# Attention with one group of products per chunk, every engine in its written order, splits a unit later and moved decoding

## The chip, the cores and the metric

One core of a Trainium2 chip runs the whole kernel as one program. The time is that of the device from start to end, in microseconds (us), median of several runs. TensorE (PE) does matrix products and transposes, VectorE (DVE), ScalarE (ACT) and GpSimd (POOL) work on elements, and SyncE (SP) issues most of the DMA transfers. Each engine runs its instructions in the order in which they stand, and waits on semaphores for the others.

## The reference

An attention over 2 batches, 8 heads, 576 positions and 64 features, followed by a dense layer with softplus, and by a mixture of 8 experts. Only the attention is touched by the change:

```python
q_rot, k_rot = (rotate(q), rotate(k))
scores = scale * np.matmul(q_rot, k_rot.transpose(0, 1, 3, 2))
scores = scores - np.max(scores, axis=-1, keepdims=True)
attn = np.exp(scores)
attn = attn / (np.sum(attn, axis=-1, keepdims=True) + 1e-09)
return np.matmul(attn, v).astype(np.float32)
...
x = np.ascontiguousarray(attn_out.transpose(0, 2, 1, 3)).reshape(B * S, H * D)
x = _moe_ref(x=x, **moe_kwargs)
return _moe2_ref(x=x, **moe2_kwargs)
```

rotate is the rotary embedding (RoPE) with cos and sin of the position. All arithmetic is held at float32 accuracy: where a product runs in the fast format, its operands are split into a high and a low half.

## The kernel before, in words

The attention works on 8 pairs of heads (2 batches of 4 pairs). A pair has five units: four of 128 query rows (0 to 3), each with scores for both heads, and a mixed unit "m", which holds the last 64 rows of both heads in one block. In batch 0 a pair's units come as 0, 1, 2, 3, m, in batch 1 as 2, 3, m, 0, 1. Two chunks of units share the product with the values: in batch 0 the units 0 and 1 (256 columns wide) and 2, 3 and m (320 wide); in batch 1 the units 2 and 3, and m, 0 and 1.

For a unit and a head, TensorE makes the scores s (s_mm, L261; L243 for the mixed one), VectorE takes the maximum m (s_max, L270), ScalarE the exponential P with its sum (s_exp, L283). One unit later TensorE transposes P in three blocks of three (t_steps, L352; the mixed unit has one block of four and one of one), and ScalarE or VectorE copies each block into pt (L96, L98). When a chunk's blocks are there, TensorE multiplies them with the values into pv (pv_mm, L396). The sums become reciprocals (norm, L304, L305), are spread along a row into R, are transposed (norm_out, L316), copied to rb (norm_in), and pv times rb is x (x_out, L405), which GpSimd splits into the halves xh and xl for the next layer.

Meanwhile the next pair is made ready: GpSimd does its RoPE (L134 to L137), TensorE transposes q and k (tq, L174), ScalarE takes the high half out of PSUM (L161, L165) and VectorE the low half (L220, called from do_later), and SyncE copies both into the stacked forms qs and ks by DMA (L227). In batch 1 weights of the next layer are also loaded and decoded (decode, L557 to L560 on VectorE; high, L565 on ScalarE; low, L569 on VectorE), at units given in the table W_AT.

What sets the order: the string ORDER gives the steps of one unit's turn (S scores, T transposes, M maximum, E exponential, H copies of blocks, J products, N scaling, K and L the low halves, W weights, Q preparation of the next pair), and PREP what Q does in each of the five turns of a pair. Within a turn the four engines TensorE, VectorE, ScalarE and SyncE keep the written order; GpSimd is left to the scheduler, and each turn is a section of its own. The transposes, q and k transposes and R transposes share a pool of three PSUM buffers (tag t); scores have two, pv has one.

Of the kernel before, what the change touches and what calls it, by code (L numbers as in the profile page):

```python
# [27 lines left out]
ORDER = "S0 R T0 M0 K H0 E0 S1 T1 M1 L E1 H1 W J T2 N H2 Q".split()  # L28

PREP = (("xR", "k", "q", "xvR", ""), ("k", "qR", "x", "vm", ""), ("k", "qR", "x", "v", "r"))  # L30
# [11 lines left out]
    ((0, 0), (18, 24, 25, 25, 26)), ((0, 1), (20, 26, 27, 27, 28)), ((1, 0), (25, 28, 29, 29, 30)),  # L42
    ((1, 1), (27, 30, 31, 31, 32)), ((2, 0), (29, 32, 33)), ((3, 0), (31, 34, 35)), ((2, 1), (33, 36, 37)),
# [16 lines left out]
class Attention:  # L60


    def __init__(self, tc, q, k, v, cst, xh, xl, pools):
# [3 lines left out]
        self.engines = {nc.tensor.engine, nc.vector.engine, nc.scalar.engine, nc.sync.engine}  # L67
        self.pr = {}
        self.rem, self.rot = {}, {}
# [61 lines left out]
    def _rope(self, engs, out, x, tmp, cos, sin):  # L131

        e1, e2, e3 = engs
        e1.tensor_mul(out, x, cos)  # L134
        e2.tensor_mul(tmp[..., 0:32], x[..., 32:64], sin[..., 0:32])
        e2.tensor_mul(tmp[..., 32:64], x[..., 0:32], sin[..., 32:64])
        e3.tensor_add(out, out, tmp)  # L137

    def rope_rem(self, b, engs):
        self.rot[b] = self.nat.tile([128, H, D], F32, name=f"remr{b}", tag="remr", bufs=1)  # L140
        tmp = self.nat.tile([128, H, D], F32, name=f"remt{b}", tag="rtmp", bufs=2)
        c, s = (self.cst[x].unsqueeze(1).to_broadcast([128, H, D]) for x in ("cosr", "sinr"))
        self._rope(engs, self.rot[b], self.rem[b], tmp, c, s)

    def rope_pair(self, b, hp, i, engs):
        p = self.pr[b, hp]
        if "rot" not in p:
            p["rot"] = self.nat.tile([128, 2, 4, 2, D], F32, name=f"rot{b}{hp}", tag="rot", bufs=1)
        tmp = self.nat.tile([128, 2, 4, D], F32, name=f"rt{b}{hp}{i}", tag="rtmp", bufs=2)
# [3 lines left out]
        rot = p["rot"][:, i].rearrange("p j h d -> p h j d")  # L153
        self._rope(engs, rot, p["xn"][:, i], tmp, c, s)
# [145 lines left out]
    def norm(self, b, hp, c):  # L300
# [18 lines left out]
    def norm_in(self, b, hp, c, ps):  # L319
# [9 lines left out]
        self.x_out(b, hp, c)  # L329
# [70 lines left out]
    def x_out(self, b, hp, c):  # L400
# [26 lines left out]
    def run(self, side=None):  # L427
# [7 lines left out]
        with self.tc.manual_schedule(engines=self.engines):  # L435
            self.warm(0)
            for i in range(2):
                self.rope_pair(0, 0, i, (nc.vector,) * 3)
                self.tq(0, 0, i)
                self.warm(1 + i)  # L440
            self.rope_rem(0, (nc.vector,) * 3)
            low_q, _, low_k, _ = self.later
            self.later = []
            low_q()
            low_k()
            self.tr(0, True)
            self.warm(3)
        units = [(b, hp, u) for (b, hp) in pairs for u in self.order[b]]
        n = len(units)
        jobs = []  # L450
        for i in range(n + 4):
# [4 lines left out]
            with self.tc.manual_schedule(engines=self.engines):  # L456
                for step in ORDER:
                    g = int(step[1]) if len(step) > 1 else 0
# [5 lines left out]
                    elif step[0] == "S" and act:  # L464
                        self.s_mm(*cur, g)
                        if (i, g) == (0, 1):
                            self.warm(4)
# [948 lines left out]
def attention_moe_moe_kernel(ctx: ExitStack, tc, q, k, v, w_in, w_out, w_skip, w_gate, w1, w2, tab, out):  # L1416
    nc = tc.nc
# [205 lines left out]
```

## Time and profile before

| | |
|---|---|
| time, median of 3 runs | 493.01 us (492.19 to 493.56) |
| profiled execution | 493.06 us |
| its span | 491.2 us |
| mean granted TensorE clock | 0.998 |
| PE busy | 471.3 us (96%) |
| DVE busy | 371.8 us (76%) |
| ACT busy | 332.3 us (68%) |
| POOL busy | 130.6 us (27%) |
| attention, first scores to first hidden product | 12.65 to 165.1 us |

The durations in the rows are those of one profiled execution; the span leaves out some 1.9 us around it. A row of the time line gives start and duration of one instruction, or of several alike merged (x4), and in brackets how long the engine idled before it and who released it. One f32 product shows as two matmuls. A matmul's end is modelled, so what one piece costs TensorE is read from the start of one row to the start of the next. Rows of the mixed unit start a "pair" here: the mixed unit's scores of pair 0 stand at 28.44 us, of pair 3 at 82.91, of pair 4 (the first of batch 1) at 92.99, and of the last pair at 149.11. In rows 1 below the columns are: stretch, its length, then PE, PEld, DVE, ACT and POOL busy (us, with the instructions), the granted clock, the DMA share and GB/s.

### The profile page before, as it was taken

Reading aid. Unit: us, or ns where it says so; the run is one execution under the profiler, and the core shown is the slowest. Engines: PE = TensorE matmul, PEld = TensorE weight load, DVE = VectorE, ACT = ScalarE, POOL = GpSimd, SP = SyncE. Lnnn points to the kernel's source line nnn. Section 1 sums busy time; section 2 is a strip of 40 time slices with the busy share of each in tenths; the row PEclk is TensorE's granted clock in tenths of the full one; section 3 lists DMA queues with packets and bytes.
Section 4 is the critical chain, followed back from the end, with each engine's and each line's share of the span. In section 5 each row is a group of like instructions: output and inputs, shape, how many; then the busy total and the mean of one; then the engine's idle time right before and its main releaser. Section 6 shows DMA issues by size and latency. Waiting matters only on the chain. (4 is left out here: it accounts for less than half of the span.)

```text
span 491.2 us, 8838 instructions
## 1 busy us (share of the span) xinstructions
PE 471.3 (96%) x3054; PEld 382.1 (78%) x3055; DVE 371.8 (76%) x699; ACT 332.3 (68%) x782; POOL 130.6 (27%) x166
## 2 busy tenths in 40 slices
PE   7999999999999999999999999999999999999994
PEld 3777777766777678999998898899897768677683
DVE  7666776688996796799988995454886688979563
ACT  2667776676877677876678677765685458957550
POOL 0966785766131400000000000000110152551002
PEclk9999999999999999999999999999999999999999
DMA  7477547458462240223344241420335545895231
GB/s 186 152 194 195 121 123 200 95 161 208 101 177 77 97 129 1 87 63 113 125 129 125 91 129 44 140 75 2 99 100 203 228 111 194 285 311 224 78 120 39
DMA packets 41509, 65.49 MB, mean 133 GB/s; under 512 B 9087, under 2 KB 23679, under 8 KB 41456
## 3 DMA queue, kind: packets, MB, share of 16 engines
q1 hardware_dynamic: 38480, 59.99, 40.0%
q0 software_dynamic: 1344, 4.20, 2.7%
q10 hardware_dynamic: 1632, 0.66, 0.6%
q8 instruction: 26, 0.43, 0.4%
q14 instruction: 27, 0.22, 0.1%
HBM read 67.32 MB, written 6.76 MB: 151 GB/s over the span
## 5 line engine op out<-in xcount | busy, mean ns | idle before, releaser
L591 PE MATMUL h<-xh,w 128*128 128x320 f32 (+2 forms) x464 | 104.2, 309 | 0.8 <-ACT rb L96 0.8
L629 PE MATMUL acc<-w,gh 128*128 128x512 f32 x288 | 80.8, 397 | 1.3 <-ACT gh L619 1.3
L591 PEld LDWEIGHTS h<-xh,w 128*128 128x128 f32 x464 | 78.1, 188 | 4.7 <-ACT rb L96 1.1
L591 PE MATMUL h<-xl,w 128*128 128x320 f32 (+2 forms) x232 | 69.2, 308 | 0.0
L270 DVE TENSOR_REDUCE m<-s 128x1 f32<-128x576 f32 x64 | 48.0, 754 | 19.5 <-PE s L261 16.1
L629 PEld LDWEIGHTS acc<-w,gh 128*128 128x128 f32 x288 | 51.8, 188 | 12.0 <-ACT gh L619 3.2
L283 ACT ACTIVATE P<-s,m 128x576 f32<-128x576 f32 x64 | 47.6, 749 | 12.3 <-DVE m L270 10.7
L705 POOL TENSOR_SCALAR sc<-lg 128x2 f32<-128x2 f32 (+1 forms) x3 | 0.9, 293 | 201.8 <-DVE lg L688 201.8
L973 DVE TENSOR_TENSOR ws<-raw,ws 128x1024 fp32r<-128x1024 f32 x42 | 49.4, 1219 | 6.6 <-ACT ws L966 6.1
L604 ACT ACTIVATE y<-h 128x320 f32<-128x320 f32 (+2 forms) x58 | 25.4, 438 | 41.1 <-PE h L591 39.9
L352 PE MATMUL t<-ct,P 128*128 128x128 f32 x288 | 45.5, 277 | 2.5 <-ACT pt L96 2.5
L629 PE MATMUL acc<-w,gl 128*128 128x512 f32 x144 | 45.9, 392 | 0.0
L966 ACT CAST ws<-raw 128x1024 fp32r<-128x1024 f32 x42 | 42.0, 1051 | 5.2 <-DMA raw<-in_moe_w_dram 5.0
L620 DVE TENSOR_TENSOR gl<-r,gh 128x256 fp32r<-128x256 f32 (+2 forms) x42 | 25.8, 614 | 26.0 <-ACT gh L619 25.8
L261 PE MATMUL s<-ks,qs 128*128 128x288 f32 x224 | 43.7, 317 | 1.8 <-ACT P L283 1.7
L591 PEld LDWEIGHTS h<-xl,w 128*128 128x128 f32 x232 | 43.2, 188 | 2.0
L352 PEld LDWEIGHTS t<-ct,P 128*128 128x128 f32 x288 | 33.6, 140 | 9.6 <-issue 3.5
L96 ACT COPY pt<-t 128x384 f32<-128x384 f32 x60 | 28.1, 480 | 18.0 <-PE t L352 17.9
L396 PE MATMUL pv<-pt,vr 128*64 128x256 f32 (+1 forms) x256 | 37.1, 412 | 0.0
L638 PE MATMUL y<-ws,hT 128*128 128x512 f32 (+1 forms) x150 | 37.0, 392 | 0.0
L261 PEld LDWEIGHTS s<-ks,qs 128*128 128x128 f32 x224 | 31.6, 189 | 6.6 <-ACT P L283 3.6
L638 PE MATMUL mh<-ws,xgT 128*128 128x512 f32 x132 | 36.6, 418 | 0.0
(305 smaller groups left out, 946.1 us busy)
## 6 DMA issues: line engine op xcount, KB each, us to landing
raw<-in_moe_w_dram SPq DMA_DIRECT2D x56, 512.0 KB
raw<-in_moe_w_in_dram SPq DMA_DIRECT2D x16, 512.0 KB
raw<-in_moe_w_out_dram SPq DMA_DIRECT2D x16, 512.0 KB
sraw<-in_moe_w_dram SPq DMA_DIRECT2D x16, 512.0 KB
ks<-kT SPq DMA_DIRECT2D x28, 288.0 KB
qs<-qT SPq DMA_DIRECT2D x28, 128.0 KB
wr<-in_moe_w_dram SPq DMA_DIRECT2D x5, 512.0 KB
x2d<-x SPq DMA_DIRECT2D x9, 256.0 KB
```

The costliest lines, as they stand in the source:

```text
L96: self.nc.scalar.copy(out, in_)
L261: nc.tensor.matmul(ps[:, c, 0:288], lhsT=qs[:, a, uc], rhs=ks[:, a, x, 288 * c : 288 * c + 288], start=x == 0, stop=x == 1,)
L270: self.last = nc.vector.tensor_reduce(st["m"][:, a : a + 1], st["ps"][a][:, :, 0:288], axis=AX.XY, op=ALU.max, negate=True)
L283: nc.scalar.activation(P[:, 576 * a : 576 * a + 576].rearrange("p (c n) -> p c n", c=2), ps[:, :, 0:288], AF.Exp, bias=m[:, a : a + 1], ac ...
L352: self.tail = nc.tensor.transpose(ps[:, 128 * i : 128 * i + 128], src, ident)
L396: nc.tensor.matmul(ps[r, 0:n], lhsT=v, rhs=pt[:, k, 0:n], start=i < 0, stop=i == 3, skip_group_check=True,)
L591: nc.tensor.matmul(ps[c][:, 0:m], lhsT=w[:, 0, x, 128 * k : 128 * k + 128], rhs=src[:, k, c0 + m * c : c0 + m * c + m], start=z == 0, stop ...
L620: self.last = nc.vector.tensor_sub(gl, r, gh.bitcast(F32))
L629: nc.tensor.matmul(acc[t], lhsT=g[x][:, 128 * j : 128 * j + 128], rhs=w[:, 1, y, :], start=f == f0 and z == 0, stop=f == f1 and z == 2,)
L638: mm()
L966: self.nc.scalar.copy(self.w[T, c][:, 0], self.raw[c] if raw is None else raw)
L973: self.nc.vector.tensor_sub(w[:, 1], self.raw[c] if raw is None else raw, w[:, 0].bitcast(F32))
```

## The change

- The products of a chunk stand in one group in one turn (step J), followed by the transposes of the reciprocals. Before, they stood as two half groups in two turns, with a block of transposes behind the first half.
- All three blocks of transposes stand ahead of J, and the copies H1 and H2 too.
- The scaling (N and X) comes at the start of the next turn, and the split into xh and xl (Y) a turn after that.
- VectorE instead of GpSimd spreads the reciprocals into R.
- RoPE of a coming pair is cut into its single instructions, and the table ROPE says how many of them each turn takes (step G); the rotated q and k have two buffers instead of one. The q transposes stand one turn later (PREP).
- The turns of decoding and loading (W_AT) are others, and decoding stands whole in one turn.
- One section of written order holds the whole attention, and GpSimd is in it too.

```diff
-ORDER = "S0 R T0 M0 K H0 E0 S1 T1 M1 L E1 H1 W J T2 N H2 Q".split()
-
-PREP = (("xR", "k", "q", "xvR", ""), ("k", "qR", "x", "vm", ""), ("k", "qR", "x", "v", "r"))
+ORDER = "S0 R N T0 Y G M0 X K H0 E0 S1 T1 T2 M1 L E1 H1 H2 W J Q".split()
+
+PREP = (("xR", "k", "q", "xvR", ""), ("k", "R", "qx", "vm", ""), ("k", "R", "qx", "v", "r"))
+
+ROPE = ((0, 8, 0, 0, 4), (2, 2, 2, 2, 4), (2, 2, 2, 2, 0))
...
-    ((0, 0), (18, 24, 25, 25, 26)), ((0, 1), (20, 26, 27, 27, 28)), ((1, 0), (25, 28, 29, 29, 30)),
-    ((1, 1), (27, 30, 31, 31, 32)), ((2, 0), (29, 32, 33)), ((3, 0), (31, 34, 35)), ((2, 1), (33, 36, 37)),
+    ((0, 0), (18, 23, 23, 24, 26)), ((0, 1), (20, 26, 26, 27, 28)), ((1, 0), (24, 28, 28, 29, 31)),
+    ((1, 1), (27, 31, 31, 32, 33)), ((2, 0), (29, 33, 33)), ((3, 0), (32, 36, 36)), ((2, 1), (34, 38, 38)),
...
-        self.engines = {nc.tensor.engine, nc.vector.engine, nc.scalar.engine, nc.sync.engine}
+        self.engines = {nc.tensor.engine, nc.vector.engine, nc.scalar.engine, nc.sync.engine, nc.gpsimd.engine}
...
-        e1.tensor_mul(out, x, cos)
-        e2.tensor_mul(tmp[..., 0:32], x[..., 32:64], sin[..., 0:32])
-        e2.tensor_mul(tmp[..., 32:64], x[..., 0:32], sin[..., 32:64])
-        e3.tensor_add(out, out, tmp)
+        return [
+            lambda: e1.tensor_mul(out(), x, cos),
+            lambda: e2.tensor_mul(tmp()[..., 0:32], x[..., 32:64], sin[..., 0:32]),
+            lambda: e2.tensor_mul(tmp()[..., 32:64], x[..., 0:32], sin[..., 32:64]),
+            lambda: e3.tensor_add(out(), out(), tmp()),
+        ]
...
+                p["rot"] = self.nat.tile([128, 2, 4, 2, D], F32, name=f"rot{b}{hp}", tag="rot", bufs=2)
...
+    def ropes(self, n=None):
+
+        for _ in range(len(self.off) if n is None else min(n, len(self.off))):
+            self.off.pop(0)()
...
-            self.cp("g", R[:, 64 * k0 : 64 * k0 + k * d].rearrange("p (a d) -> p a d", a=k), x)
+            self.cp("v", R[:, 64 * k0 : 64 * k0 + k * d].rearrange("p (a d) -> p a d", a=k), x)
...
-        self.x_out(b, hp, c)
...
-    def pv_mm(self, b, hp, c, z):
+    def pv_mm(self, b, hp, c):
         nc, p, pt, n = self.nc, self.pr[b, hp], self.pt[b, hp, c], self.width(b, c)
-        if z == 0:
-            self.pv[b, hp, c] = self.ps_pv.tile([128, 512], F32, name=f"pv{b}{hp}{c}", tag="pv")
-        ps = self.pv[b, hp, c]
-        for i in ((-1, 0, 1), (2, 3))[z]:
+        ps = self.pv[b, hp, c] = self.ps_pv.tile([128, 512], F32, name=f"pv{b}{hp}{c}", tag="pv")
+        for i in range(-1, 4):
...
+        return partial(self.x_split, x, xh, xl)
+
+    def x_split(self, x, xh, xl):
         self.cp("g", xh, x)
-        nc.gpsimd.tensor_sub(xl, x, xh.bitcast(F32))
...
+        jobs, scale, split = [], None, []
+        for i in range(n + 2):
             cur = units[i] if i < n else None
             prev = units[i - 1] if 0 < i <= n else None
-            T, evs, scale = None, [None] * 3, None
+            T, evs = None, [None] * 3
...
+                if step == "R":
+                    T = self.t_steps(*prev) if prev else None
+                    if ready:
+                        self.norm(*ready[0])
...
+                elif step == "J" and ready:
+                    job = ready.pop(0)
+                    self.pv_mm(*job)
+                    scale = self.norm_out(*job)
+                    if i >= n:
                         scale()
-                    elif step in "KL":
-                        if (step == "K") == (0 < i < 5):
-                            self.do_later()
-                    elif step == "W" and side:
-                        side(i)
-                    elif step == "Q" and cur:
-                        self.prepare(i, pairs)
-                        if i == 1:
-                            self.warm(5)
+                        self.x_out(*job)()
+                        scale = None
+                elif step == "G":
+                    self.ropes(ROPE[min(i // 5, 2)][i % 5])
+                elif step == "Y" and split:
+                    split.pop()()
+                elif step == "N" and scale:
+                    scale()
+                elif step == "X" and scale:
+                    split.append(self.x_out(*scale.args[:3]))
+                    if i >= n:
+                        split.pop()()
+                    scale = None
...
-                        jobs += [(b, hp, c, z) for z in range(2)]
-        assert not jobs
+                        jobs.append((b, hp, c))
...
+                self.off += self.rope_pair(*nx, 1, g3) + self.rope_pair(*nx, 0, g3)
...
-            att.run(side)
+            with tc.manual_schedule(engines=att.engines):
+                att.run(side)
```

Three places show how the instructions move. The first is TensorE from the second scores of unit 1 (the first row) in the pair after "01m", batch 0: t is a block of transposes, pv the products, t01n the transposes of reciprocals, tq the q transposes. Before:

```order
L261 MATMUL s_812<-ks_513,qs_574 128x288 x4
L352 MATMUL t_817<-ct,P_766 128x128 x3
L396 MATMUL pv_829<-pt_654,vd_105 64x320 x2
L396 MATMUL pv_829<-pt_654,vr_127 64x320 x4
L352 MATMUL t_836<-ct,P_766 128x128 x3
L261 MATMUL s_863<-ks_513,qs_574 128x288 x4
L174 MATMUL tq_841<-ct,rot_576 128x128 x4
L352 MATMUL t_868<-ct,P_810 128x128 x3
L261 MATMUL s_878<-ks_513,qs_574 128x288 x4
L352 MATMUL t_883<-ct,P_810 128x128 x3
L396 MATMUL pv_829<-pt_654,vr_127 64x320 x4
L316 MATMUL t01n_899<-ct,R_800 128x128 x3
```

and in the changed kernel, from the same scores:

```order
L287 MATMUL s_776<-ks_493,qs_603 128x288 x4
L377 MATMUL t_781<-ct,P_731 128x128 x3
L377 MATMUL t_785<-ct,P_731 128x128 x3
L419 MATMUL pv_798<-pt_613,vd_105 64x320 x2
L419 MATMUL pv_798<-pt_613,vr_129 64x320 x8
L342 MATMUL t01n_809<-ct,R_762 128x128 x3
L287 MATMUL s_813<-ks_493,qs_603 128x288 x4
L377 MATMUL t_822<-ct,P_774 128x128 x3
L287 MATMUL s_838<-ks_493,qs_603 128x288 x4
L377 MATMUL t_843<-ct,P_774 128x128 x3
L377 MATMUL t_847<-ct,P_774 128x128 x3
L200 MATMUL tq_855<-ct,rot_568 128x128 x4
```

The third block (t_836 before, t_785 now) went from behind the first products to ahead of them, and the second half of the products from behind unit 2's blocks into the one group.

The second is ScalarE at the same place: the exponential of unit 0's second head, the small copies of the mixed block (t01m), the cast of the k transposes, then the first block's copy and unit 1's exponentials. Before:

```order
L283 ACTIVATE P_766,sm_767<-s_769,m_762 128x576
L96 COPY pt_654<-t01m_774 64x64 x2
L165 CAST kT_785<-tq_780 128x512
L96 COPY pt_797<-t_803 128x3x128
L283 ACTIVATE P_810,sm_767<-s_792,m_807 128x576
L283 ACTIVATE P_810,sm_767<-s_812,m_807 128x576
L96 COPY pt_797<-t_836 128x3x128
L161 ACTIVATE qT_846<-tq_841 128x512
```

and now:

```order
L309 ACTIVATE P_731,sm_732<-s_734,m_727 128x576
L98 COPY pt_613<-t01m_739 64x64 x2
L191 CAST kT_750<-tq_745 128x512
L98 COPY pt_759<-t_765 128x3x128
L309 ACTIVATE P_774,sm_732<-s_754,m_771 128x576
L309 ACTIVATE P_774,sm_732<-s_776,m_771 128x576
L98 COPY pt_759<-t_785 128x3x128
L98 COPY rb_818<-t01n_809 128x256
```

The rows up to the copy of the third block (t_836, t_785) stand alike; behind it the scaling's copies rb follow, and the q activation, which stood there, comes a turn later.

The third is VectorE from the mixed unit's maximum on (m01m), with the copy of a block, the reciprocals, x, and the copies of the mixed block. Before:

```order
L270 TENSOR_REDUCE m01m<-s01m_709 128x1
L98 COPY pt_654<-t_726 128x3x128
L304 TENSOR_SCALAR sm_603<-sm_603 128x5
L305 RECIPROCAL sm_603<-sm_603 128x5
L270 TENSOR_REDUCE m_762<-s_752 128x1
L405 TENSOR_TENSOR x_744<-pv_680,rb_742 128x256
L98 COPY pt_654<-t01m_757 128x4x64 x2
L270 TENSOR_REDUCE m_762<-s_769 128x1
```

and now:

```order
L296 TENSOR_REDUCE m01m<-s01m_675 128x1
L428 TENSOR_TENSOR x_695<-pv_653,rb_682 128x256
L100 COPY pt_613<-t_701 128x3x128
L296 TENSOR_REDUCE m_727<-s_711 128x1
L100 COPY pt_613<-t01m_716 128x4x64 x2
L296 TENSOR_REDUCE m_727<-s_734 128x1
L330 TENSOR_SCALAR sm_578<-sm_578 128x5
L331 RECIPROCAL sm_578<-sm_578 128x5
L100 COPY R_762<-sm_578 128x256
L100 COPY R_762<-sm_578 128x128
```

x now stands right behind the mixed maximum, the reciprocals moved behind the maxima of unit 0, and two new copies to R follow them.

## Rows read from the trace of the kernel before

**Rows 1.** Stretches of the attention and of what follows: busy time of each engine.
```profile
28.44:82.91 54.47, 52.47 (x404) 40.77 (x402) 39.65 (x76) 40.22 (x107) 38.78 (x53) 1.00 0.61 157
82.91:92.99 10.08, 9.61 (x75) 7.42 (x72) 7.92 (x16) 6.72 (x18) 5.15 (x10) 1.00 0.30 88
92.99:149.11 56.12, 52.69 (x396) 39.87 (x393) 47.92 (x91) 41.44 (x108) 26.55 (x35) 1.00 0.64 168
149.11:165.10 15.99, 15.02 (x114) 10.37 (x111) 10.44 (x23) 11.39 (x30) 3.50 (x7) 1.00 0.11 34
165.10:460.00 294.90, 292.75 (x1752) 249.82 (x1753) 231.31 (x437) 210.23 (x478) 34.72 (x34) 1.00 0.39 129
```

**Rows 2.** Waits of PE in the attention: us in total, times, longest.
```profile
PE t L352 <- ACT pt L96: 2.5, 3, 1.0
```

**Rows 3.** Time line of PE around products of a chunk.
```profile
54.24 0.76 PE L396 MATMUL pv<-pt,vd 128*64 128x320 f32 x4
...
56.01 0.55 PE L352 MATMUL t<-ct,P 128*128 128x128 f32 x3
...
57.36 0.49 PE L352 MATMUL t<-ct,P 128*128 128x128 f32 x3
57.61 0.78 PE L261 MATMUL s<-ks,qs 128*128 128x288 f32 x4
58.23 0.49 PE L352 MATMUL t<-ct,P 128*128 128x128 f32 x3
58.65 1.30 PE L396 MATMUL pv<-pt,vr 128*64 128x320 f32 x8
59.88 0.55 PE L316 MATMUL t01n<-ct,R 128*128 128x128 f32 x3
...
160.87 0.76 PE L396 MATMUL pv<-pt,vd 128*64 128x320 f32 x4
...
163.71 0.55 PE L316 MATMUL t13n<-ct,R 128*128 128x128 f32 x3
```

**Rows 4.** Time line of DVE, ACT and PE behind the mixed unit of pair 0.
```profile
29.51 0.76 DVE L270 TENSOR_REDUCE m00m<-s00m 128x1 f32<-128x576 f32 x1 [0.16 <-PE s00m L243]
30.36 0.74 ACT L283 ACTIVATE P00m<-s00m,m00m 128x576 f32<-128x576 f32 x1
...
34.53 0.74 ACT L283 ACTIVATE P<-s,m 128x576 f32<-128x576 f32 x1 [0.83 <-DVE m L270]
35.41 0.80 PE L261 MATMUL s<-ks,qs 128*128 128x288 f32 x4 [0.54 <-ACT P L283]
35.70 0.58 ACT L165 CAST kT<-tq 128x512 fp32r<-128x512 f32 x1
36.18 0.48 ACT L96 COPY pt<-t 128x384 f32<-128x384 f32 x1
```

**Rows 5.** Groups of DVE in the attention: busy us, mean ns, idle before.
```profile
L98 DVE COPY pt<-t 128x384 f32<-128x384 f32 x36 | 19.6, 548 | 3.1 <-PE t L352 3.1
...
L405 DVE TENSOR_TENSOR x<-pv,rb 128x256 f32<-128x256 f32 x8 | 3.3, 409 | 0.1
...
L98 DVE COPY pt<-t01m 128x256 f32<-128x256 f32 x2 | 0.7, 412 | 0.0
```

**Rows 6.** Time line of PE and ACT before the mixed unit of pair 0.
```profile
26.21 0.55 PE L352 MATMUL t<-ct,P 128*128 128x128 f32 x3
...
26.45 0.59 ACT L161 ACTIVATE qT<-tq 128x512 fp32r<-128x512 f32 x1
```

**Rows 7.** Time line of POOL and DVE; the adds' durations: ns min/median/max.
```profile
85.67 0.73 POOL L135 TENSOR_TENSOR rt<-xn,cr 128x256 f32<-128x256 f32 x1 [2.53 <-DMA xn<-in_k_dram]
...
85.70 0.73 DVE L304 TENSOR_SCALAR sm<-sm 128x5 f32<-128x5 f32 x1 [0.49 <-ACT P03m L283]
...
L304 DVE TENSOR_SCALAR sm<-sm x16: 157/170/730, 19.9 to 159.3; 128x4 f32<-128x4 f32 x8, 128x5 f32<-128x5 f32 x8
```

**Rows 8.** SyncE's DMA issues of the stacked q.
```profile
59.07 3.81 SPq L227 DMA_DIRECT2D qs<-qT  x4
```

More of the change, by code (lines that the diff above doesn't have):

```diff
@@ L152, in rope_pair @@
         )
-        rot = p["rot"][:, i].rearrange("p j h d -> p h j d")
-        self._rope(engs, rot, p["xn"][:, i], tmp, c, s)
+        return self._rope(engs, out, p["xn"][:, i], tmp, c, s)
+    def ropes(self, n=None):
+        for _ in range(len(self.off) if n is None else min(n, len(self.off))):
+            self.off.pop(0)()
     def halves(self, hi, lo, src, q=False):
@@ L405, in x_out @@
         nc.vector.tensor_mul(x, ps[:, 0:n], self.rb[b, hp, c][:, 0:n])
+        return partial(self.x_split, x, xh, xl)
+    def x_split(self, x, xh, xl):
         self.cp("g", xh, x)
-        nc.gpsimd.tensor_sub(xl, x, xh.bitcast(F32))
+        self.nc.gpsimd.tensor_sub(xl, x, xh.bitcast(F32))
     def warm(self, part):
@@ L434, in run @@
         self.load_v(*pairs[1])
[L435 to L447, printed above, removed]
+        self.warm(0)
@@ L448, in run @@
+        for i in range(2):
+            some(self.rope_pair(0, 0, i, (nc.vector,) * 3))
+            self.tq(0, 0, i)
+            self.warm(1 + i)
+        some(self.rope_rem(0, (nc.vector,) * 3))
+        low_q, _, low_k, _ = self.later
+        self.later = []
+        low_q()
+        low_k()
+        self.tr(0, True)
+        self.warm(3)
         units = [(b, hp, u) for (b, hp) in pairs for u in self.order[b]]
         n = len(units)
-        jobs = []
-        for i in range(n + 4):
+        jobs, scale, split = [], None, []
@@ new lines, in run @@
+            for step in ORDER:
+                g = int(step[1]) if len(step) > 1 else 0
+                act = cur and (g == 0 or cur[2] != "m")
+                if step == "R":
+                    T = self.t_steps(*prev) if prev else None
+                    if ready:
+                        self.norm(*ready[0])
+                elif step[0] == "S" and act:
+                    self.s_mm(*cur, g)
+                    if (i, g) == (0, 1):
+                        self.warm(4)
+                elif step[0] == "M" and act:
+                    self.s_max(*cur, g)
+                elif step[0] == "E" and act:
+                    self.s_exp(*cur, g)
+                elif step[0] == "T" and T and T[g]:
+                    evs[g] = T[g]()
+                elif step[0] == "H" and evs[g]:
+                    evs[g]()
+                elif step == "J" and ready:
[3 more added lines that the diff above has]
+                    if i >= n:
+                        scale()
+                        self.x_out(*job)()
[11 more added lines that the diff above has]
+                    scale = None
+                elif step in "KL":
+                    if (step == "K") == (0 < i < 5):
+                        self.do_later()
+                elif step == "W" and side:
+                    side(i)
+                elif step == "Q" and cur:
+                    self.prepare(i, pairs)
+                    if i == 1:
+                        self.warm(5)
@@ L495, in run @@
                     if ch[-1] == u:
-                        jobs += [(b, hp, c, z) for z in range(2)]
-        assert not jobs
+                        jobs.append((b, hp, c))
+        assert not jobs and not split and not scale and not self.off
     def prepare(self, i, pairs):
@@ L521, in prepare @@
             if step == "r" and n2 == (1, 0):
+                assert 1 in self.rot
                 self.tr(1)
```

54 lines of the change are left out of this document (18 added, 36 removed).

## The prediction, made before the changed kernel ran

> **What bounds the kernel now.** I read the mean clock and the stretches first, then TensorE's waits, then its rows in order. The granted clock is 1.00 in every stretch [rows 1], so no part of this is a clock matter. From 165.1 to 460 us TensorE is busy 292.75 of 294.90 us: whatever time the attention part saves or loses reaches the end one for one, since the instructions behind it stand in the same order as before. In the attention part the reader sees 52.47 of 54.47 us busy for three pairs of heads, and 52.69 of 56.12 us for the last three, where VectorE is at 47.92: the first are bound by TensorE, the last also by VectorE, which decodes weights there. TensorE's longest sum of waits in the attention part is 2.5 us, for ScalarE's copies of transposed blocks [rows 2]; its idle time from 28.44 to 165.1 us is 2.0, 0.5, 3.4 and 1.0 in the four stretches [rows 1], some 7 us. So the change can win what TensorE does not have to do, and part of these 7 us, and can lose whatever cover its new order takes from the chains of VectorE and ScalarE.
>
> **One group of products: the gain.** In one pair the products of a 320-wide chunk take 1.77 us for the first group (54.24 to 56.01) and 1.23 for the second (58.65 to 59.88), 3.00 together; the last chunk of the kernel, whose two groups already stand back to back, takes 2.84 (160.87 to 163.71) [rows 3]. Joining saves 0.16. Three transposes ahead of products cost 0.42 (58.23 to 58.65), ahead of scores 0.25 (57.36 to 57.61): one such change of kind goes, 0.17, and one behind a group (56.01 is followed 0.30 later), 0.05. That is 0.38 a chunk, and 15 of the 16 chunks have it: 5.7 us of TensorE's work.
>
> **The waits that the order makes.** Before, each half group stood between transposes and scores of other units and covered the chains of the other two engines. Now a unit with products holds all of them at its end and the others hold none. I walk one pair of batch 0 from the mixed unit's scores at 0. Durations: its maximum starts 1.07 later and its exponential 0.85 after that; TensorE may use an exponential 0.88 after its start (34.53 to 35.41); an exponential and two small copies take ScalarE 1.17 (34.53 to 35.70), a cast 0.48, and a copy is free for TensorE 0.55 after its start (0.48 and an estimated 0.07) [rows 4]. An ordinary maximum starts 0.8 after its scores (1.07 less the two products that the mixed unit has more, an estimate), and its exponential 0.78 after that. VectorE takes 0.76 for a maximum [rows 4], 0.55 and 0.41 for a block's and a mixed block's copy, 0.41 for x [rows 5], each some 0.07 less in a queue (the cast and the copy after it overlap by 0.1).
> - TensorE: scores 0.87, nine transposes 0.75, scores of unit 0 to 2.24. The mixed block's transposes need its exponential: 1.92 + 0.88 = 2.80. Wait 0.55.
> - VectorE in its written order: mixed maximum 1.07, x 1.75, copy 2.09, maximum 2.57, two copies of the mixed block 3.44 (0.64 after its transposes), second maximum 4.14. Its exponential starts at 4.92 and the second scores of unit 1 at 5.80, where TensorE has been free since 5.25. Wait 0.55.
> - ScalarE behind that exponential: two small copies, the cast of k at 6.09, and only at 6.57 the copy of unit 0's first block. The third block takes that one's buffer, since the three buffers of this pool hold this block, the second one and the k transposes whose low half is still to come. So it starts at 7.12 and not at 6.67. Wait 0.45. Before, the half group stood ahead of this block and hid it.
> - Then products, 7.54 to 10.38, and three transposes of reciprocals to 10.68.
> - From there to the next mixed unit the same walk gives waits of 0.05 (first scores of unit 3), 0.2 (its first block, for VectorE's copy behind x and a maximum), 0.1, and 0.4 (its third block, for the copy behind the q activation), and ends at 18.5.
> Three pairs: 18.5 twice, and 19.5 for the third, where 1.0 us of casts of the remainder stands ahead of two exponentials: 56.5 against 54.47, **+2.0**. The piece up to batch 1: 10.7 against 10.08, **+0.6** [rows 1].
>
> **Batch 1.** The same walk gives some 18.3 a pair, of it 2.1 waits: 0.3 for the q transposes (buffer), 0.7 for the scores behind the unit in which VectorE decodes (busy until about 7.8), 0.8 for a first block that waits for ScalarE's copy of the unit before, 0.3 for two others. The last pair has no q and k transposes, 17.5. Together 54.1 against 56.12, **-2.0**: here the moved decoding does help, since it now stands in units with products.
>
> **Start.** In pair 0 the q activation waits for the last scores that read the old q, which end where the transposes of 26.21 us follow, and runs at 26.45 [rows 6]. It now stands ahead of the copy whose buffer the third block needs: 26.45 + 0.48 + 0.55 = 27.48, where the block would have followed at 26.46 (26.21 and 0.25). Then 0.42, the whole group (320-wide 2.84, so 256-wide about 2.3) and 0.22: the mixed unit starts at 30.4, against 28.44, **+1.9**; its share of the products is back at the end.
> **End.** From the last mixed unit to the first hidden product 15.99 before. The last copies now come as in the walk, products at 11.4 to 14.25, and the first hidden product 1.38 after (163.71 to 165.10): 15.6, **-0.4**.
>
> **Costed at nothing.** Spreading reciprocals on VectorE: no row shows such a copy; from below it is nothing, from above 0.55, the copy of a larger block out of PSUM [rows 5], 24 times at most 13 us of VectorE; I take 0.3, 7 us. They stand in the units with products, where VectorE waits for TensorE; uncovered they would cost 0.3 to 0.6 a chunk. There GpSimd stands in the way: a 5-wide add took VectorE 0.73 us, from 85.70 to 86.43, while a GpSimd multiply ran from 85.67 to 86.40; the median of these adds is 0.17 [rows 7], so it waited 0.56. I allow the same for a spread: two in a chunk stay under the 2.84 of the products. The splits a unit later, RoPE in pieces and its second buffer: GpSimd is 26.55 of 56.12 busy, 38.78 of 54.47 earlier, less the spreads now; what waits for it (q and k transposes) comes over 4 us later by the walk. If not, each of 14 would cost up to one piece. The first raw loads leave the crowded start; nobody on TensorE waited there.
>
> The Trainium skill says in "SBUF — State Buffer", section Who interferes with whom, that a VectorE operation in a two-port mode and a GpSimd operation block each other fully, whoever starts first. By that rule, with which the trace's 0.73 us agrees, the new spreads, if they are copies in such a mode, each wait for GpSimd's current piece; with the measured wait of 0.56 on 24 of them it is an estimated 13 us of VectorE's time, which speaks against the change wherever the products do not cover it, and would bring the sum to rival 4.
>
> **Sum.** 1.9 + 2.0 + 0.6 - 2.0 - 0.4 = +2.1 us on the profiled execution's 493.06 (span 491.2 and 1.9 around it; the median shown is 493.01): **495.2 us**. The 5.7 of work saved are in it; about 8 us of new or longer waits eat them. Its own range is 493.5 to 497.5.
>
> **Rivals.**
> 1. *The cover holds (faster).* If the buffers or the copies come 0.4 us earlier than I walk, the waits stay near today's 7 us and the work saved stays: 493.06 - 5.7 = 487.4; with half of it 490.2. For it: TensorE is the bound in batch 0, and each wait that I found is only 0.1 to 0.55. Against: the written order of ScalarE, in which the needed copy stands last. It decides at a third block that starts right behind the second.
> 2. *No change that can be told.* The same balance with waits 1 to 2 us smaller: 493 to 494.
> 3. *The q copies come late (slower by more).* Four of them take SyncE 3.81 us after the low half [rows 8], which is now made a unit later: the walk has it at 16.4 to 17.3, the next pair's second scores at 21.6, so the last copy, issued until about 20 to 21, has a margin of a microsecond at best. A VectorE held by GpSimd in that unit uses it up: 1.5 us at each of four pairs, 501. For it: VectorE's reciprocals now stand ahead of two maxima there. Against: SyncE's issues before were slow since the k copies were right ahead of them.
> 4. *The spreads are uncovered:* 24 times 0.3, half of it on the path, 3.6: 498.8.
>
> **Chances.** Forecast 0.38; rival 1 0.30; rival 2 0.18; rival 3 0.08; rival 4 0.06. A measurement of this kernel cannot tell 0.3% (1.5 us) from no change. The forecast's own range reaches a little into that band, so same 0.22, faster 0.30, slower 0.48. The range from 489.0 to 499.0 takes in half of rival 1's way and rival 4.
>
> **What would show it.** Right: products in one run of some 2.8 and 2.3 us; waits of transposes for ScalarE's copies grow from 2.5 us to about 8, at the third block of the units with products; pairs of batch 0 of 18.5 us, of batch 1 of 18.3; waits of the products for x are gone; the mixed unit of pair 0 starts near 30.4. Wrong: pairs of batch 0 at 17.3 or less, or the third block right behind the second; scores that wait for the copies of q.

## The result, and the profile after

The changed kernel takes 498.21 us (497.94 to 498.45), 1.0107 times the time before [1.0089, 1.0124]: 5.2 us slower, where 2.1 had been forecast. The profiled execution took 498.0 us, with a span of 495.8 and a mean granted clock of 0.995. Of the changed kernel the stretches (columns as in [rows 1]) are three pairs of batch 0, the piece to batch 1, batch 1, the end, and the rest:

```profile
30.01:86.81 56.80, 53.14 (x402) 41.24 (x402) 43.71 (x84) 39.05 (x105) 35.97 (x43) 1.00 0.56 142
86.81:98.40 11.59, 10.18 (x75) 7.57 (x74) 7.07 (x15) 7.06 (x19) 7.41 (x9) 1.00 0.68 195
98.40:154.92 56.52, 51.55 (x396) 40.43 (x394) 50.47 (x99) 40.96 (x108) 22.08 (x28) 1.00 0.59 153
154.92:170.00 15.08, 13.60 (x102) 9.57 (x100) 12.09 (x27) 10.68 (x28) 2.46 (x4) 1.00 0.24 71
170.00:465.00 295.00, 292.76 (x1753) 249.88 (x1754) 232.05 (x438) 210.89 (x480) 34.79 (x34) 1.00 0.39 129
```

Behind the attention nothing changed: TensorE has 292.76 us of work in 295.00, and had 292.75 in 294.90 [rows 1]. The first hidden product stands at 170.28 instead of 165.1, and these 5.2 us account for the difference (the two profiled executions are 4.9 us apart). By stretches:

| | before | forecast | measured |
|---|---|---|---|
| mixed unit of pair 0 at | 28.44 | 30.4 (+1.9) | 30.01 (+1.6) |
| three pairs of batch 0 | 54.47 | 56.5 (+2.0) | 56.80 (+2.3) |
| piece to batch 1 | 10.08 | 10.7 (+0.6) | 11.59 (+1.5) |
| three pairs of batch 1 | 56.12 | 54.1 (-2.0) | 56.52 (+0.4) |
| to the first hidden product | 15.99 | 15.6 (-0.4) | 15.36 (-0.6) |

Start, batch 0 and end came near what was walked. What failed is batch 1, by 2.4 us, and the piece ahead of it, by 0.9. TensorE's longest waits in the attention (us in total, times, longest), to be read against [rows 2]:

```profile
PE s L287 <- ACT P L309: 4.9, 7, 1.4
PE t L377 <- ACT pt L98: 2.4, 6, 0.6
PE s L287 <- DMA qs<-qT: 0.8, 1, 0.8
```

The unit with products in the pair of [rows 3], TensorE's time line:

```profile
49.43 1.15 PE L377 MATMUL t<-ct,P 128*128 128x128 f32 x9
50.33 0.77 PE L287 MATMUL s<-ks,qs 128*128 128x288 f32 x4
51.37 0.66 PE L377 MATMUL t01m<-ct,P01m 128*128 128x128 f32 x4 [0.27 <-ACT P01m L309]
...
54.40 0.80 PE L287 MATMUL s<-ks,qs 128*128 128x288 f32 x4 [0.44 <-ACT P L309]
55.04 0.49 PE L377 MATMUL t<-ct,P 128*128 128x128 f32 x3
55.70 0.55 PE L377 MATMUL t<-ct,P 128*128 128x128 f32 x3 [0.17 <-ACT pt L98]
56.18 0.76 PE L419 MATMUL pv<-pt,vd 128*64 128x320 f32 x4
56.77 2.32 PE L419 MATMUL pv<-pt,vr 128*64 128x320 f32 x16
59.02 0.55 PE L342 MATMUL t01n<-ct,R 128*128 128x128 f32 x3
```

The joined group takes 2.84 us (56.18 to 59.02), as forecast. The third block starts 0.66 us behind the second, where 0.33 is the way without a wait (nine transposes ahead of scores take 0.90 us, 49.43 to 50.33, and three 0.25 [rows 3]): 0.33 lost, of which the wait view shows 0.17, since it counts from a matmul's modelled end. Counted from start to start, the transposes' waits for ScalarE's copies come to an estimated 4 to 5 us instead of the view's 2.4. That is still not the 8 that I had announced, for in batch 1 the third block starts almost without a wait. There the six transposes ahead of the products take 0.80 us, and 0.75 would be the way without one (0.33 and the 0.42 of [rows 3]):

```profile
113.13 0.87 PE L377 MATMUL t<-ct,P 128*128 128x128 f32 x6
113.93 0.76 PE L419 MATMUL pv<-pt,vd 128*64 128x320 f32 x4
```

In batch 1, behind the joined products of a unit with 256 columns (TensorE in pairs 4, 5 and 6, then VectorE in pair 6):

```profile
106.56 0.82 PE L377 MATMUL t<-ct,P 128*128 128x128 f32 x6
108.20 0.79 PE L287 MATMUL s<-ks,qs 128*128 128x288 f32 x4 [0.82 <-ACT P L309]
...
125.24 0.82 PE L377 MATMUL t<-ct,P 128*128 128x128 f32 x6
127.48 0.80 PE L287 MATMUL s<-ks,qs 128*128 128x288 f32 x4 [1.42 <-ACT P L309]
...
144.52 0.82 PE L377 MATMUL t<-ct,P 128*128 128x128 f32 x6
146.75 0.79 PE L287 MATMUL s<-ks,qs 128*128 128x288 f32 x4 [1.41 <-ACT P L309]
```

```profile
140.16 1.41 DVE L296 TENSOR_REDUCE m<-s 128x1 f32<-128x576 f32 x2
141.49 0.67 DVE L246 SCALAR_TENSOR_TENSOR qT<-tq,qT 128x512 fp32r<-128x512 f32 x1
142.09 0.45 DVE L100 COPY pt<-t12m 64x64 f32<-64x64 f32 x2
142.56 0.69 DVE L605 TENSOR_TENSOR w<-wt,w 128x512 fp32r<-128x512 f32 x1
143.18 0.42 DVE L593 TENSOR_SCALAR wt<-raw 128x512 uint32<-128x512 uint32 x1
143.63 0.69 DVE L594 SCALAR_TENSOR_TENSOR wt<-raw,wt 128x512 uint32<-128x512 uint32 x1
144.36 0.69 DVE L596 SCALAR_TENSOR_TENSOR wt<-raw,wt 128x512 uint32<-128x512 uint32 x1
145.08 0.76 DVE L296 TENSOR_REDUCE m<-s 128x1 f32<-128x576 f32 x1
```

The decoding occupies VectorE up to 145.05, 8.7 us behind the mixed scores at 136.36. The next unit's scores had been there since about 143.7, their maximum comes at 145.08, and the scores after it wait 1.41 us.

### The profile page after: what moved, and what is told of

Read it like the earlier page. It is cut to its first block, busy times and chain, and to the rows that moved or that the text cites. A ratio compares the mean times of both kernels' runs of the same rounds, so it can differ in the third digit from the quotient of the medians.

```text
span 495.8 us, 8827 instructions
## 1 busy us (share of the span) xinstructions
PE 470.6 (95%) x3055; PEld 383.0 (77%) x3055; DVE 381.7 (77%) x723; ACT 331.6 (67%) x782; POOL 121.0 (24%) x142
## 4 chain that ended last, share of the span: by engine, by line
PE 71%; DVE 13%; ACT 5%; DMA 4%; issue 3%; SPq 1%; POOL 1%; POOLq 0%; DVEq 0%; ACTq 0%
PE acc L665 18%; PE h L627 17%; PE mh L674 8%; PE y L674 7%; PE pv L419 5%; DVE m L296 3%; PE t L377 3%; PE s L287 3%; ACT P L309 2%; PE lgp L721 1%; PE s L281 1%; DVE pt L100 1%; PE ht L1089 1%; DVE R L100 1%; ACT pt L98 1%
## 5 line engine op out<-in xcount | busy, mean ns | idle before, releaser
L377 PE MATMUL t<-ct,P 128*128 128x128 f32 x288 | 43.1, 277 | 3.6 <-ACT pt L98 2.4
L419 PE MATMUL pv<-pt,vr 128*64 128x256 f32 (+1 forms) x256 | 33.8, 406 | 0.0
```

What stands on the lines that cost most here:

```text
L377: self.tail = nc.tensor.transpose(ps[:, 128 * i : 128 * i + 128], src, ident)
L419: nc.tensor.matmul(ps[r, 0:n], lhsT=v, rhs=pt[:, k, 0:n], start=i < 0, stop=i == 3, skip_group_check=True,)
```

## Experiments

All are timed against the kernel before on the same chip. "Start" is the mixed unit of pair 0; batch 0, piece and batch 1 are the stretches of the table.

**Parts of the change undone or done alone.** First, the spreads on GpSimd again:

```diff
-            self.cp("v", R[:, 64 * k0 : 64 * k0 + k * d].rearrange("p (a d) -> p a d", a=k), x)
+            self.cp("g", R[:, 64 * k0 : 64 * k0 + k * d].rearrange("p (a d) -> p a d", a=k), x)
```

> The changed kernel with the reciprocals spread by GpSimd again. Theory A: the 24 spreads on VectorE (0.53 us each on average, up to 0.84 where GpSimd is at work) stand on VectorE's full path in batch 1 and make scores wait for exponentials; then batch 1 (first mixed scores of pair 4 to those of pair 7) falls from 56.5 to about 54 us, batch 0 by at most 0.5 us, the wait of scores for exponentials from 4.9 to about 2 us, and the time from 498.2 to 495 to 496. Theory B: where the decoding stands holds batch 1, and the spreads lie under the products; then 497.5 to 498.5. Theory C: the spreads on GpSimd come too late for the transposes behind the products; then over 499.

497.95 us, ratio 1.0099 [1.0085, 1.0114]: no gain, so Theory A falls, and B's number fits. Batch 0 and the piece fall by 0.8 each: in batch 0 a wait of 0.6 us for VectorE's low half of k goes, in the piece the one for the stacked q. Batch 1 rises by 1.2. VectorE and GpSimd at the decoding show why:

```profile
122.32 1.72 DVE L605 TENSOR_TENSOR w<-wt,w 128x512 fp32r<-128x512 f32 x1
```

```profile
122.21 1.28 POOL L140 TENSOR_TENSOR rot<-rot,rt 128x512 f32<-128x512 f32 x1
```

The low half of a weight takes 1.72 us instead of 0.69 while GpSimd adds: the hold-up went from the spread to the decoding.

The decoding at the turns of before:

```diff
-    ((0, 0), (18, 23, 23, 24, 26)), ((0, 1), (20, 26, 26, 27, 28)), ((1, 0), (24, 28, 28, 29, 31)),
+    ((0, 0), (18, 24, 25, 25, 26)), ((0, 1), (20, 26, 27, 27, 28)), ((1, 0), (25, 28, 29, 29, 30)),
...
```

> The changed kernel with the turns of loading and decoding (W_AT) of the kernel before. Theory A (spreads on VectorE): no gain, 498 to 500, since VectorE's load in batch 1 stays about 50.5 of 56.5 us. Theory B (a whole decoding ahead of two maxima makes the next scores wait 1.4 us): batch 1 falls from 56.5 to about 54 us and the time to 495.5 to 496.5.

502.73 us, 1.0187 [1.0170, 1.0204]: batch 1 takes 61.27. The new turns are worth 4.5 us here. B falls as it was put, and the time lies above A's range too.

The third block behind the products:

```diff
-ORDER = "S0 R N T0 Y G M0 X K H0 E0 S1 T1 T2 M1 L E1 H1 H2 W J Q".split()
+ORDER = "S0 R N T0 Y G M0 X K H0 E0 S1 T1 M1 L E1 H1 W J T2 H2 Q".split()
```

> The changed kernel with the third block of transposes and its copy behind the products again. Theory A (the third block ahead of the products waits 0.4 us for a copy's buffer in each unit with products, and starts pair 1 to 4 later in the first pair): about 1 us off the start, 0.4 to 0.8 off each pair of batch 0, less in batch 1, which VectorE sets: 495 to 496.5. Rival: the block only fills time that the following unit needs anyway for its maxima, and the wait comes back there: 497.5 to 498.5. If its copy then comes late for the next products: over 499.

496.55 us, 1.0064 [1.0051, 1.0077], at the edge of A's range: start at 29.27, batch 0 54.99 instead of 56.80. Batch 1 loses 1.1, where scores now wait twice for the stacked q, 2.3 us in all.

The kernel before with only the products joined:

```diff
-        for i in ((-1, 0, 1), (2, 3))[z]:
+        for i in ((-1, 0, 1, 2, 3), ())[z]:
```

> The kernel before with only the products joined: all products of a chunk stand in the turn of the first half, the transposes of the reciprocals stay a turn later. Theory A: joining saves 0.16 us and some of the switches a chunk, 2.5 to 4 us in all, but its second half no longer covers ScalarE and VectorE in the next turn: 489.5 to 492. Rival: the cover is worth what the joining saves, 492 to 494. If cover is the larger part: 495 or more.

498.74 us, 1.0126 [1.0108, 1.0144]: joining alone costs 5.5 us, 1.4 in batch 0 and 4.5 in batch 1 (60.66). TensorE, where before eight products stood between the first two of these rows:

```profile
117.43 0.49 PE L352 MATMUL t<-ct,P 128*128 128x128 f32 x3
117.87 0.52 PE L316 MATMUL t10n<-ct,R 128*128 128x128 f32 x3
118.23 0.49 PE L352 MATMUL t<-ct,P 128*128 128x128 f32 x3
119.36 0.63 PE L352 MATMUL t11m<-ct,P11m 128*128 128x128 f32 x4 [0.64 <-DVE pt L98]
119.74 0.77 PE L261 MATMUL s<-ks,qs 128*128 128x288 f32 x4
121.17 0.33 PE L352 MATMUL t11m<-ct,P11m 128*128 128x128 f32 x1 [0.65 <-ACT rb L96]
```

The 1.2 us of the half group are gone, and waits stand in their place: the 0.64 us are new, and the 0.65 had been 0.26 (the wait of the next products for x, 0.66 before, fell to 0.26). The half group had covered VectorE's and ScalarE's copies.

**Is it the joining?** The changed kernel with half groups, with the third block ahead and behind:

```diff
-        for i in range(-1, 4):
+        for i in ((-1, 0, 1), (2, 3))[z]:
...
-                        jobs.append((b, hp, c))
+                        jobs += [(b, hp, c, z) for z in range(2)]
```

> The changed kernel with the products in two half groups over two turns again, all else as changed (third block ahead of the products, spreads on VectorE, new decoding turns, one written section). Theory A (the joined group takes the products out of two turns of five, and there the two maxima and the two exponentials set the pace): batch 1 falls from 56.5 to 53 or 54 us, batch 0 from 56.8 to about 55.5, and the time to 493.5 to 495.5. Theory B (the third block's buffer and VectorE's spreads are what costs): no gain, 497.5 or more, since joining saves TensorE work.

> The changed kernel with half groups and with the third block and its copy behind the products. Theory A: about 1 us below the run with halves alone, as the block behind the products took 1.7 us off the joined kernel (batch 0 at 54.5): 492 to 494. If the halves already cover the buffer wait, the same as that run.

506.77 and 503.73 us (1.0269 [1.0254, 1.0283], 1.0217): slower by far, so the theory that half groups would give the loss back falls. Batch 0, where nothing is decoded, is slower too: 56.72 us in the second, against 54.99 for the joined products with the block behind. In batch 1 of the second (63.5 us) decoding meets GpSimd's RoPE, VectorE and GpSimd:

```profile
117.40 1.65 DVE L597 SCALAR_TENSOR_TENSOR wt<-raw,wt 128x512 uint32<-128x512 uint32 x1
```

```profile
117.16 1.33 POOL L140 TENSOR_TENSOR rot<-rot,rt 128x512 f32<-128x512 f32 x1
```

How much of batch 1's loss such hold-ups are was not measured. Each grouping of the products is slow in the order made for the other.

The kernel before with only the new table W_AT (the second experiment's edit the other way round), and the changed one with a written section per turn:

```diff
-            for step in ORDER:
+            with self.tc.manual_schedule(engines=self.engines):
+                for step in ORDER:
...
-            with tc.manual_schedule(engines=att.engines):
-                att.run(side)
+            att.run(side)
```

> The kernel before with only the new turns of loading and decoding. In the changed kernel these turns are worth 4.5 us (498.2 against 502.7 with the old ones). Theory A (they repair what the joining broke: they put the decoding into turns that have products, and before every turn but one has some): no gain here, 492.5 to 495. Theory B (they are better in any order): 489 to 491, batch 1 at 52 to 54 instead of 56.1.

> The changed kernel with a section of written order per turn, as before, so that instructions of neighbouring turns may pass each other. Theory A (the loss is from the joined products, not from the single section): 497 to 499.5. Rival (before, scores of the next turn went ahead of products, and the single section forbids it): 494 to 496.

493.93 us (1.0014 [1.0005, 1.0023]) and 498.84 (1.0112 [1.0097, 1.0128]), both as A: the new turns bring nothing by themselves, and the single section is not the cause.

**Batch 1.** GpSimd's RoPE of the last two pairs replaced by copies:

```diff
+        if b == 1 and hp > 1:
...
+            return [partial(self.copy_raw, b, hp, i)]
```

> The changed kernel, where for the last two pairs of heads SyncE copies q and k unrotated and GpSimd does no RoPE in batch 1 (this leaves out the rotation of these two pairs). Theory A (in batch 1 VectorE sets the pace, 54.7 of 56.5 us, and GpSimd's RoPE holds up spreads and decoding there, some 1 us a pair): pairs 4 and 5 fall by 0.5 to 1 us each, pair 6, which has no RoPE before, stays at 18.6; time 496.5 to 497.5. Theory B (the chain from maximum to exponential to scores, not GpSimd): pairs 4 and 5 as they are, 498 to 498.5.

574.18 us, most of it behind the attention, on other data; batch 1 took 59.86. SyncE's four copies (4.35 us) stand ahead of those of q, and scores wait for q three times, 5.3 us. It tells nothing on the question.

Spreads on ScalarE, then also the third block behind the products in batch 0 (LATE is the order of the third experiment), and spreads on ScalarE in the kernel before:

```diff
-            self.cp("v", R[:, 64 * k0 : 64 * k0 + k * d].rearrange("p (a d) -> p a d", a=k), x)
+            self.cp("a", R[:, 64 * k0 : 64 * k0 + k * d].rearrange("p (a d) -> p a d", a=k), x)
...
-            for step in ORDER:
+            for step in ORDER if i >= 20 else LATE:
...
-            self.cp("g", R[:, 64 * k0 : 64 * k0 + k * d].rearrange("p (a d) -> p a d", a=k), x)
+            self.cp("a", R[:, 64 * k0 : 64 * k0 + k * d].rearrange("p (a d) -> p a d", a=k), x)
```

> The changed kernel with the reciprocals spread by ScalarE. Theory A (VectorE's 5.6 us of spreads in batch 1 are on the path, and on GpSimd they only moved the hold-up to the decoding): batch 1 falls from 56.5 to 53.5 to 55 us, the piece from 11.6 to 10.8, and the time to 494.5 to 496.5. Theory B (ScalarE's written order is what is late, and a spread ahead of copies and exponentials makes it later): 498 to 500.

> Spreads on ScalarE, and in batch 0 the third block and its copy behind the products. Theory A: the start (0.7 us) and batch 0 (1.8 us) gained by the block behind the products add to what the spreads on ScalarE bring: 2 to 2.5 us below that run, 492 to 494. Theory B (the two gains fill the same waits): within 0.7 us of that run.

> The kernel before with the reciprocals spread by ScalarE instead of GpSimd. If GpSimd's spreads hold VectorE up (add and decoding, an estimated 1 to 2 us in batch 1 where VectorE is at 53.0 of 56.1): 491 to 492.5. If ScalarE's order pays for it: 493.5 to 495.

The first: 500.34 us, 1.0142 [1.0127, 1.0158], so A falls, and the time lies a little above B's range. Batch 1 stays, 56.73, though VectorE now has 3.5 us less to do:

```profile
31.89:90.41 58.52, 53.27 (x403) 41.21 (x402) 38.45 (x75) 41.14 (x114) 35.88 (x43) 1.00 0.55 139
101.67:158.40 56.73, 51.84 (x395) 40.38 (x394) 46.94 (x90) 43.12 (x117) 21.92 (x28) 1.00 0.58 150
```

In batch 1 the three waits behind the decoding shrink by 0.27 us each, but in pairs 4 and 5 the third block now waits some 0.5 us for ScalarE's copy (its six transposes take 1.31 us at 116.13, where they took 0.80), and the two cancel. Batch 0 rises to 58.52: a longer ScalarE queue makes the third block wait more. With the block behind the products (second kernel) batch 0 falls by 4.2 us to 54.29, the start from 31.89 to 29.28, and the time to 494.84, 1.0034 [1.0021, 1.0048]: 5.5 us, where 2 to 2.5 were expected. This bears the forecast's mechanism out: the third block ahead of the products waits for a buffer that ScalarE's last copy frees. The third: 494.19 us, 1.0015 [1.0006, 1.0024], no gain.

Three decodings taken out of the table; and two low halves moved from turns 28 and 33 to 31 and 36:

```diff
-    ((1, 1), (27, 31, 31, 32, 33)), ((2, 0), (29, 33, 33)), ((3, 0), (32, 36, 36)), ((2, 1), (34, 38, 38)),
+    ((1, 1), (27, 31, 31, 32, 33)),
...
-    ((0, 0), (18, 23, 23, 24, 26)), ((0, 1), (20, 26, 26, 27, 28)), ((1, 0), (24, 28, 28, 29, 31)),
-    ((1, 1), (27, 31, 31, 32, 33)), ((2, 0), (29, 33, 33)), ((3, 0), (32, 36, 36)), ((2, 1), (34, 38, 38)),
+    ((0, 0), (18, 23, 23, 24, 26)), ((0, 1), (20, 26, 26, 27, 31)), ((1, 0), (24, 28, 28, 29, 31)),
+    ((1, 1), (27, 31, 31, 32, 36)), ((2, 0), (29, 33, 33)), ((3, 0), (32, 36, 36)), ((2, 1), (34, 38, 38)),
```

> The changed kernel with the last three entries of the decoding table left out, so that these weights are loaded and decoded behind the attention. Read from the mixed scores of pair 6 to those of pair 7, where two of these decodings stood (18.56 us). Theory A (2.5 us of decoding behind the last maximum of the unit with 256-wide products make the next unit's scores wait 1.4 us): 17.0 to 17.4 us there, pairs 4 and 5 as they were. Theory B (TensorE's waits for copies and for the third block set the pair): 18.2 to 18.6. The whole time says little, since the decoding then falls on the hidden layer.

> The changed kernel with two low halves of weights (0.69 us each on VectorE) moved from the units with 256-wide products (turns 28 and 33) to the next with 320-wide products (turns 31 and 36), where VectorE idles 0.5 to 1.1 us before the mixed maximum. Theory A: the wait of scores behind turns 28 and 33 falls from 1.4 to 0.7 us, pairs 5 and 6 to 18.6 and 17.9, and the time to 496.5 to 497.3. Theory B: 498 to 498.5; if turn 31 then makes the mixed maximum late: the same, with the wait moved.

Without the entries (503.49 us, 1.0223) pair 6 took 24.1 instead of 18.56: left to the scheduler, the decodings stand among its maxima all the same, two at a time. The edit did not do what it was meant to. With the low halves moved (498.07, 1.0101 [1.0084, 1.0118]) pair 6 falls from 18.56 to 17.97, as A expects, but pair 5 does not, and the time neither: scores now wait for the stacked q, in total, times and longest:

```profile
PE s L287 <- DMA qs<-qT: 3.6, 3, 1.4
```

The same low halves moved in the kernel of 494.84 us, and then the third block behind the products everywhere:

```diff
-            for step in ORDER if i >= 20 else LATE:
+            for step in LATE:
```

> Spreads on ScalarE, in batch 0 the third block behind the products (494.8 before), and the two low halves moved. Theory A: both gains add, 493.2 to 494. Theory B: the moved halves bring nothing here, 494.5 to 495.

> As the kernel with spreads on ScalarE and moved low halves, with the third block behind the products in batch 1 too. Theory A (there it still waits 0.3 us a pair for a copy, and 0.5 to 0.9 in the piece to batch 1): 491.5 to 493.5. Theory B (in batch 1 VectorE sets the pace): within 0.5 us of that kernel.

493.74 us (1.0018 [1.0008, 1.0028]): pairs 5 and 6 go from 19.51 and 18.30 to 18.91 and 17.71, so 0.69 us of decoding less behind the last maximum is worth 0.6 a pair, and A holds. Then 491.82 us, 0.9979 [0.9970, 0.9988], 0.2% faster than the kernel before and 1.3% faster than the changed one: the piece takes 10.37, batch 1 54.38.

```profile
29.88:84.18 54.30, 51.95 (x404) 41.37 (x402) 38.96 (x75) 40.84 (x115) 35.86 (x43) 1.00 0.62 159
84.18:94.55 10.37, 9.66 (x75) 7.53 (x74) 7.39 (x14) 7.12 (x20) 7.33 (x9) 1.00 0.64 179
94.55:148.93 54.38, 51.52 (x395) 40.53 (x394) 46.87 (x90) 43.15 (x117) 21.85 (x28) 1.00 0.61 160
```

Last, this kernel with the spreads on VectorE ("a" to "v"), and with half groups (the edit shown for them above):

> The best kernel so far (third block behind the products everywhere, low halves moved, spreads on ScalarE: 491.8) with the spreads on VectorE. Theory A (VectorE's spreads stand 2.4 us where GpSimd's rotation runs, as in the run with the block behind, and then scores wait for the stacked q): 1 to 3 waits of scores for q of 0.5 to 1.4 us, 493.5 to 496. Theory B (who spreads makes no difference, as between 498.2 and 497.95 on VectorE and GpSimd): 491.5 to 492.5.

> The best kernel so far with the products in two half groups over two turns. Theory A (joining saves TensorE 0.38 us a chunk, which shows only once the waits are gone): 2 to 5 us more than 491.8 from the work alone, pairs of batch 0 at 18.2. Theory B (half groups cover the waits as in the kernel before): 490 to 492, pairs of batch 0 at 17.5. In batch 1 the decoding then meets GpSimd's rotation as in the runs with halves, and 496 to 502 would come from there.

496.21 us (1.0070 [1.0055, 1.0084]): now VectorE's spreads cost 4.4 us. Two spreads at 90.85 take 2.44 us, like those of the changed kernel shown further down, and scores wait twice for q:

```profile
PE s L288 <- DMA qs<-qT: 1.7, 2, 0.9
```

With half groups 505.33 us (1.0251 [1.0237, 1.0265]), above every range given, and pairs of batch 0 at 18.7 against 17.8: joining is worth 0.9 us a pair in this order, but half groups were not given an order of their own.

## Why the prediction was right and wrong

- **Right: the third block, the start and batch 0.** The walk gave 18.5, 18.5 and 19.5 us for the pairs, the trace 18.54, 18.54 and 19.72; 30.4 against 30.01 for the start. The cause, a buffer that ScalarE's last copy frees, is shown by the block behind the products (1.8 us off batch 0) and by a longer ScalarE queue (1.7 us more). That 18.5 came to the tenth is partly luck: in the pair at 48.55 the waits come to an estimated 2.1 us where the walk had 2.3, and nine transposes take 0.90 where it had 0.75.
- **Wrong: batch 1, "-2.0: here the moved decoding does help".** The term that failed is the wait of "0.7 for the scores behind the unit in which VectorE decodes (busy until about 7.8)": it was taken too small. VectorE is busy until 8.1 us behind the mixed scores in pair 4 and until 8.7 in pairs 5 and 6. From the start of the six transposes to the start of these scores TensorE takes 1.64, 2.24 and 2.23 us, and without a wait an estimated 0.57 (three take 0.25, nine 0.90). So the waits, counted as in the walk, are some 1.1, 1.7 and 1.7 us (the view shows 0.82, 1.42 and 1.41), 4.4 in place of 2.1: nearly all of the 2.4 us. The runs show what lengthened VectorE's queue. The same stretch of TensorE, with batch 1 as a whole (the third kernel has the block behind in batch 0 too):

| | pair 4 | pair 5 | pair 6 | batch 1 |
|---|---|---|---|---|
| changed kernel | 1.64 | 2.24 | 2.23 | 56.52 |
| spreads on ScalarE | 1.37 | 1.97 | 1.97 | 56.73 |
| and the low halves moved | 1.37 | 1.37 | 1.37 | 55.54 |
| and the third block behind the products everywhere | 1.36 | 1.31 | 1.30 | 54.38 |

The spread ahead of the maxima costs 0.27 us each time, and the low half of a weight ahead of the decoding 0.6 in pairs 5 and 6. Without both VectorE is done at 7.8 us, as walked (120.72, with the mixed scores at 112.90), and the wait is an estimated 0.74. In the last kernel, TensorE and then VectorE in pair 5:

```profile
121.12 0.82 PE L378 MATMUL t<-ct,P 128*128 128x128 f32 x6
122.43 0.80 PE L288 MATMUL s<-ks,qs 128*128 128x288 f32 x4 [0.49 <-ACT P L310]
```

```profile
120.03 0.69 DVE L597 SCALAR_TENSOR_TENSOR wt<-raw,wt 128x512 uint32<-128x512 uint32 x1
```

Batch 1 is then 54.38 us, where 54.1 had been forecast. The 1.2 us of the table's last step are no part of the 2.4: they take away the waits of the third block that the spreads on ScalarE had brought. Against the old turns the new ones do help, by 4.5 us, but only within the joined kernel; in the kernel before, with its half groups, they bring nothing. So they seem to pay back what joining alone costs there in batch 1, 4.5 us too; that it is the same waits is not shown.
- **The spreads: mis-sized.** I took 0.3 us each, 7 us. The 24 spreads take 12.7 us (9.4 and 3.3 us in the profile's groups): 0.43 for two with GpSimd idle, 2.43 beside it. The Trainium skill ("SBUF — State Buffer", Who interferes with whom) has a VectorE copy in a two-port mode and a GpSimd operation block each other; the trace agrees that they wait. The estimate by it was 13 us of waits, and they are some 6: alone a spread takes 0.29 or 0.22 us, an estimated 6.4 for the 24. Rival 4's 498.8 lies near the measured 498.2, but not by its cause: with the spreads on GpSimd the kernel was as slow, since what batch 0 and the piece won was lost in batch 1, where the decoding was held up instead. On the path in the changed kernel were 0.27 us in each pair of batch 1 and the piece's wait for q, told next.
- **Rival 3, the late copies of q, is in part what came in the piece.** The sum had put this wait at nothing. One wait of 0.81 us stands there, behind a pair of spreads of 2.43 us, and it is gone where GpSimd or ScalarE spreads. Counted from start to start it is 1.05 (nine transposes at 87.69 and the scores at 89.64, 1.95 apart instead of 0.90), about the 0.9 by which the piece was off. In the kernels with VectorE's spreads it grew when another wait went (2.3, 3.6 and 1.7 us). VectorE and GpSimd of the changed kernel at that pair of spreads:

```profile
73.98 0.19 DVE L331 RECIPROCAL sm<-sm 128x5 f32<-128x5 f32 x1
74.21 2.43 DVE L100 COPY R<-sm 128x256 f32<-128x256 f32 x2
76.67 1.42 DVE L296 TENSOR_REDUCE m<-s 128x1 f32<-128x576 f32 x2
```

```profile
74.00 1.28 POOL L140 TENSOR_TENSOR rot<-rot,rt 128x512 f32<-128x512 f32 x1
75.24 1.32 POOL L137 TENSOR_TENSOR rot<-xn,cr 128x512 f32<-128x512 f32 x1
```

The first of the two spreads waits for GpSimd's addition to end at 75.28, the second for the multiplication behind it, to 76.56; the maxima behind them start up to 2 us later than after 0.43.
- **The gain of joining.** The 2.84 and 2.31 us of the groups are as forecast. It reaches the time nowhere by itself: in the best kernel a pair of batch 0 takes 17.8 us, as before.

## What to carry to other kernels

A half group of products between two units is also cover. Before joining such groups, write down which copies and maxima run beside each half, and price their waits in every unit that loses it; then the other engines' steps must be moved again for the new order. Where a queue is walked by hand, add up each engine's own queue up to the instruction that others wait for: here 0.3 to 0.9 us missed on VectorE, once a pair, was nearly all of the 2.4 us by which batch 1 was off.

## What the runs showed of the hardware

VectorE and GpSimd hold each other up. Of the two spreads in a row at 74.21 us, each waited for one of GpSimd's operations (2.43 us instead of 0.43). It need not be each: the two at 92.89 took 0.68, and GpSimd's addition, which starts at 93.36 beside the second, 1.35 instead of 1.28. Not only copies are held: beside GpSimd a subtraction of two 128x512 operands took 1.72 us instead of 0.69 (spreads on GpSimd), and an operation that joins shifted words 1.65 instead of 0.69 (half groups, block behind). Maxima, which read scores out of PSUM, took 0.74 to 0.76 us in the changed kernel, with GpSimd at work or idle.
